# Filter rows interleaved over the partitions of a spectral filter and token MLP kernel, and the waits for loads moved ahead of the last two stores

## The chip, the cores and the metric

The kernel runs on one core of a Trainium2 chip. The metric is the device time of one launch in microseconds (us); lower is better. Names of engines: PE is TensorE (matmul; PEld is its weight load), DVE is VectorE, ACT is ScalarE, POOL is GpSimd, SP is SyncE, which here only issues DMAs (its queue is called SPq in the profile).

## The reference

Two blocks follow each other on one input of 2048 tokens by 512 channels, bf16. The first is a global filter: a 2D real FFT, a product with a complex weight, and the inverse FFT, added to the input. The second is a token-mixing MLP with a GELU. Layer norms go ahead of both (two of them in a row ahead of the MLP).

```python
def _A_ref(x, w_r, w_i):                       # x: (1, 2048, 512)
    X = rfft2(x.astype(float32), axes=(-2, -1))
    X = X * (w_r + 1j * w_i)                   # w: (2048, 257)
    return irfft2(X, s=(S, D), axes=(-2, -1)).astype(bfloat16)

def _B_ref(x, w1, b1, w2, b2):                 # w1: (2048, 1376), w2: (1376, 2048)
    h = _layernorm(x)
    u = gelu(einsum("bsd,sf->bdf", h, w1) + b1)
    return (einsum("bdf,fs->bds", u, w2) + b2).transpose(0, 2, 1)

h  = x + _A_ref(_layernorm(x), A_w_r, A_w_i)
h2 = h + _B_ref(_layernorm(h), B_w1, B_b1, B_w2, B_b2)
```

## The kernel before

Everything is matmuls with tables of sines and cosines. A token index is 16 p + s2, with p on the 128 partitions and s2 from 0 to 15.

- Stage f1 (lines 658 to 678) transforms over p, with the layer norm's factor folded into the table FS; stage f2 (681 to 689) transforms over the channels; stage x (692 to 709) transforms over s2 with the table M and multiplies by the filter. Stages f2, x and g1 run over u from 0 to 7, four groups g of frequencies per u (lines 727 to 731).
- In stage x, two DVE multiplications of 128 x 1024 per u (line 707) read the matmul's result from PSUM and the filter tiles Wr and Wi from SBUF, and write V. Stage g1 (712 to 725) transforms V back over s2 with the table R into PQ.
- Stages g2 and g3 (lines 743 to 756) transform back over channels and p, and line 758 adds the input to make H; lines 760 to 779 are the second layer norm, which gives HH; mm1 and mm2 (736 to 741, 809 to 817) are the MLP. Line 815 makes the output tile OUT on DVE, and a DMA per s2 stores it.

The filter tiles Wr and Wi hold [128 partitions, 32 groups, 257 channels] of bf16. A partition is a row of the spectrum: a pair (k2, s), a sign (the row of a positive frequency or of its mirror), and comp, the real or imaginary part that the row of data holds. The function `_row` (line 40) says which partition that is; the tables M and R are filled with it. Before the change, the rows of positive sign lie at partitions 0 to 63, those of negative sign and comp 0 at 64 to 95, and of negative sign and comp 1 at 96 to 127. Both comps need the same filter values, so every value is loaded twice.

The filter is loaded in three blocks of groups (0 to 8, 8 to 16, 16 to 32), for Wr and then for Wi in each (lines 584 to 597): one DMA for partitions 0 to 63, whose rows are contiguous in memory (8 or 16 groups of 514 bytes), and one for each of the two quarters of 32 partitions with the mirrored rows, which run backwards in memory and so consist of pieces of 514 bytes. In the first block two small loads (`z0`, `z1`) bring the group that has no mirror. That makes 22 DMAs, all on SP's queue, behind the input X, the tables FP and EM, and ahead of the table IF, the weights W1, the biases and W2.

The order of work is made by a planner in Python (`schedule`, line 289) when the kernel is built. Each operation has an estimated duration, a priority and dependencies; the planner puts the operations in an order for each engine. A DMA's duration is its bytes over a `rate` in bytes per ns (220 for the filter, 290 or 400 for others). Dependencies come from `cells` (line 207): it turns a piece of a tile into keys of 32 or 4 bytes and a block of 32 partitions, and writers and readers of the same key depend on each other. `gen_sync` (381) turns them into semaphores; a DMA gets one of 60 semaphores of the SP queue in turn, or one of 8 of the ACT queue. `emit` (427) writes the instructions. Right before the last store, it makes SP wait for the final value of every DMA semaphore but the one of that store (62 waits, line 440), and after the store for that one.

Of the kernel before, what the change touches and what calls it, by code (L numbers as in the profile page):

```python
# [10 lines left out]
NP = 128  # L11
# [26 lines left out]


def _row(sign, comp, k2, s):  # L40
    return 64 + comp * 32 + k2 * 2 + s if sign else (k2 * 2 + s) * 2 + comp


def _fwd_matrices(special):


    m = np.zeros((64, 2, 128), np.float64)
    for s, k2, kind, sign, k2o, so in _outputs(special):
        for n in range(16):
            w = np.exp(-1j * TWO_PI * n * k2 / 16)  # L50
            if kind == 3:
                w = w * np.exp(-1j * np.pi * n / 16)
            sg = -1j if kind == 1 else 1j
            comps = {0: ((0, 1.0), (1, 1j)), 1: ((0, 1.0), (1, 1j)), 2: ((0, 1.0),), 3: ((1, 1.0),)}[kind]
            for comp, uc in comps:
                for cs, us in ((0, 1.0), (1, sg)):
                    v = w * uc * us
                    m[n * 4 + comp * 2 + s, cs, _row(sign, 0, k2o, so)] += v.real
                    m[n * 4 + comp * 2 + s, cs, _row(sign, 1, k2o, so)] += v.imag
    return m  # L60


def _inv_matrices(special):

    r = np.zeros((128, 2, 128), np.float64)

    def col(pq, n, comp, s):
        return pq * 64 + n * 4 + comp * 2 + s

    for s, k2, kind, sign, k2o, so in _outputs(special):  # L70
        for n in range(16):
            e = np.exp(1j * TWO_PI * k2 * n / 16)
            if kind == 3:
                e = e * np.exp(1j * np.pi * n / 16)
            for wri in range(2):
                jw = 1.0 if wri == 0 else (-1j if kind == 1 else 1j)
                for comp, uc in ((0, 1.0), (1, 1j)):
                    z = jw * uc * e
                    rr = _row(sign, comp, k2o, so)
                    if kind >= 2:  # L80
                        r[rr, wri, col(0, n, kind - 2, 0)] += 2.0 * z.real
                        r[rr, wri, col(1, n, kind - 2, 0)] += -2.0 * z.imag
                    else:
                        q = 1j * z * (1.0 if kind == 0 else -1.0)
                        r[rr, wri, col(0, n, 0, s)] += z.real
                        r[rr, wri, col(0, n, 1, s)] += z.imag
                        r[rr, wri, col(1, n, 0, s)] += q.real
                        r[rr, wri, col(1, n, 1, s)] += q.imag
    return r
# [62 lines left out]
def lane_quantum(lane):  # L152
    return 16 if lane.startswith("dq") else 1
# [27 lines left out]
class Builder:  # L181
# [25 lines left out]
    def cells(self, ap):  # L207
        lo, size = self.tensors[ap.tensor.name]
        esz = dt.size(ap.dtype)
        dims = list(ap.ap)  # L210
        pstep, pn = dims[0]
        row = size // esz
        off = int(ap.offset)
        p0, f0 = divmod(off, row)
        offs = np.array([f0], dtype=np.int64)
        run = 1
        for step, n in dims[1:]:
            if n == 1:
                continue
            offs = (offs[:, None] + step * np.arange(n, dtype=np.int64)[None, :]).reshape(-1)  # L220
        b = lo + offs * esz
        small = size <= 1024
        cell = 4 if small else CELL
        c = np.unique(np.concatenate([b // cell, (b + esz - 1) // cell]))
        quads = range(p0 // 32, (p0 + pn - 1) // 32 + 1)
        return [(small, q * 131072 + int(x)) for q in quads for x in c]

    def op(self, name, engines, emit, ins=(), outs=(), dur=100.0, unit=None, pr=False, pw=False,
           first=False, last=False, prio=0, nbytes=0, is_dma=False, not_before=0.0, after=(), lat=None, rate=None):
# [197 lines left out]
    def emit(self, es):  # L427
        nc = self.nc
        sems = {lane: es.enter_context(nc.semaphore(f"sem_{lane}")) for lane in sorted(self.lane_count)}
        block = es.enter_context(nc.Block())  # L430
        sec = {"sp": "sync", "pe": "tensor", "act": "scalar", "dve": "vector", "pool": "gpsimd"}
        for sname in _STREAMS:
            ops = self.streams[sname]

            def section(eng, sname=sname, ops=ops):
                for k, o in enumerate(ops):
                    if sname == "sp" and k == len(ops) - 1:
                        for lane in sorted(self.lane_count):
                            if lane.startswith("dq") and lane != o.lane:
                                eng.wait_ge(sems[lane], lane_quantum(lane) * self.lane_count[lane])  # L440
                    for lane, v in o.waits:
                        eng.wait_ge(sems[lane], v * lane_quantum(lane))  # L442
                    ins = o.emit(sname, eng, o.unit.bank if o.unit is not None else None)
                    if o.increments:
                        ins.then_inc(sems[o.lane], lane_quantum(o.lane))
                if sname == "sp":
                    eng.wait_ge(sems[ops[-1].lane], lane_quantum(ops[-1].lane) * self.lane_count[ops[-1].lane])
                    eng.nop()
            getattr(block, sec[sname])(section)

# [63 lines left out]
def build_kernel(nc, A_x, A_w_r, A_w_i, B_w1, B_b1, B_w2, B_b2, out):  # L514
# [11 lines left out]
    Wx = (T["Wr"], T["Wi"])  # L526
# [7 lines left out]
    def dma(name, dst, src, nbytes, stream="sp", outs=(), ins=(), prio=0, nb=0.0, strided=False, after=(), rate=None):  # L534
        def emit(s, eng, bank):
            if strided:
                with nc.allow_non_contiguous_dma(reason="small bias gather"):
                    return eng.dma_start(dst, src)
            return eng.dma_start(dst, src)  # L539
        return K.op(name, stream, emit, ins=ins, outs=outs, nbytes=nbytes, is_dma=True, prio=prio, not_before=nb, after=after, rate=rate)  # L540
# [33 lines left out]
    ld_x(12, 16, "act")  # L574
    ld_fp(8, 16)
    dma("ld_EM", EM[:], cin["EM"][:, :], 6656 * 128, outs=[EM[:]], prio=29)
    def w_cells(w, p0, p1, h0, h1):

        res = [Wx[w][p0:p1, h1 - 1:h1, 0:240]]
        if h1 - h0 > 1:  # L580
            res.append(Wx[w][p0:p1, h0:h1 - 1, :])
        return res

    for g0, g1 in ((0, 8), (8, 16), (16, 32)):
        n = (g1 - g0) * 257
        for w, dram in ((0, A_w_r), (1, A_w_i)):
            dma(f"ld_w{w}p_{g0}", Wx[w][0:64, g0:g1, :], bass.AP(dram.tensor, g0 * 257, [[64 * 257, 32], [0, 2], [1, n]]), 64 * n * 2,
                outs=w_cells(w, 0, 64, g0, g1), prio=28, rate=220.0)
            h0 = max(g0, 1)
            for comp in range(2):  # L590
                p0, p1 = 64 + comp * 32, 96 + comp * 32
                if g0 == 0:
                    dma(f"ld_w{w}z{comp}", Wx[w][p0:p1, 0:1, :], bass.AP(dram.tensor, 32 * 257, [[64 * 257, 32], [1, 257]]), 32 * 514,
                        outs=w_cells(w, p0, p1, 0, 1), prio=28)
                dma(f"ld_w{w}m{comp}_{g0}", Wx[w][p0:p1, h0:g1, :],
                    bass.AP(dram.tensor, (64 - h0) * 257, [[64 * 257, 32], [-257, g1 - h0], [1, 257]]),
                    32 * (g1 - h0) * 514, outs=w_cells(w, p0, p1, h0, g1), prio=28, rate=220.0)
    B1s, B1f, B2s, B2f = (T[n] for n in ("B1s", "B1f", "B2s", "B2f"))
    dma("ld_IF", IF[:], cin["IF"][:, :, :, :], 1 << 20, outs=[IF[:]], prio=27)
    w1src = B_w1.rearrange("(p s2) f -> p s2 f", s2=NS2)  # L600
# [25 lines left out]
    for i0, i1 in ((0, 2), (2, 4), (4, 6), (6, 8), (8, 10), (10, 12), (12, 14), (14, 15), (15, 16)):  # L626
# [21 lines left out]
        for i in range(i0, i1):  # L648
# [3 lines left out]
                 lambda s, eng, bank, i=i, r=r: eng.tensor_scalar(FS[:, i, :, :], FP[:, i, :, :], r, None, op0=ALU.mult),  # L652
# [6 lines left out]
    for q in range(4):  # L659
        for b in range(2):  # L660
            unit = PsumUnit("f1", 2)
            for n in range(4):
# [3 lines left out]
                f = FS[:, n2, 1, :]  # L666
# [76 lines left out]
    for s2 in range(NS2):  # L743
# [33 lines left out]
        m, r = mv[:, s2, 0:1], T["rs2"][:, s2:s2 + 1]  # L777
        K.op(f"ln2_ap{s2}", "dve", lambda s, eng, bank, m=m, r=r, hs=hs, s2=s2: eng.tensor_scalar(HH[:, s2, :], hs, m, r, op0=ALU.subtract, op1=ALU.mult),  # L778
             ins=[hs, m, r], outs=[HH[:, s2, :]], dur=320.0, prio=9)
        for t in range(5):  # L780
# [5 lines left out]
         outs=[B1f[0:96, 10:11]], dur=80.0)  # L786
# [39 lines left out]
def bass_sequential_preLN__spectral_gfnet__mixer_token_mlp__prompt_kernel(  # L826
    nc,
    A_x,
    A_w_r,
    A_w_i,  # L830
    B_x,
    B_w1,
    B_b1,
    B_w2,
    B_b2,
    out,
):
    build_kernel(nc, A_x, A_w_r, A_w_i, B_w1, B_b1, B_w2, B_b2, out)
# [28 lines left out]
```

## Time and profile before

| | us |
|---|---|
| time, median of 3 runs (lowest to highest) | 147.34 (146.84 to 148.27) |
| span of the profiled run | 145.5 |
| PE busy | 124.7 (86%) |
| DVE busy | 81.0 (56%) |
| ACT busy | 64.3 (44%) |
| mean DMA rate over the span | 156 GB/s |

A time is about 2 us longer than the span that the profile covers. The busy time of engines is an average over stages with different limits, so the stages are read one by one. A slice of the page's second part is 3.6 us:

```profile
PE   0059879999197599999999999999999999999980
DVE  0489948994349659999600369744452423233330
PEclk9999999999869999999999999999999999999998
DMA  4999999999999999997000000000012121212121
```

Each digit is the busy share of a slice in tenths; PEclk is the clock granted to TensorE, and DMA the mean share of the 16 DMA engines. The first half of the DMA row is full, up to about 65 us; the stores at the end show as 1 and 2. The PE row is full from about 55 us to the end and uneven before.

### The profile page before, as it was taken

Reading aid. Unit: us, or ns where it says so; the run is one execution under the profiler, and the core shown is the slowest. Engines: PE = TensorE matmul, PEld = TensorE weight load, DVE = VectorE, ACT = ScalarE, POOL = GpSimd, SP = SyncE. Lnnn points to the kernel's source line nnn. Section 1 sums busy time; section 2 is a strip of 40 time slices with the busy share of each in tenths; the row PEclk is TensorE's granted clock in tenths of the full one; section 3 lists DMA queues with packets and bytes.
Section 4 is the critical chain, followed back from the end, with each engine's and each line's share of the span. In section 5 each row is a group of like instructions: output and inputs, shape, how many; then the busy total and the mean of one; then the engine's idle time right before and its main releaser. Section 6 shows DMA issues by size and latency. Waiting matters only on the chain.

```text
span 145.5 us, 2043 instructions
## 1 busy us (share of the span) xinstructions
PE 124.7 (86%) x754; PEld 77.7 (53%) x754; DVE 81.0 (56%) x169; ACT 64.3 (44%) x138; POOL 18.1 (12%) x49
## 2 busy tenths in 40 slices
PE   0059879999197599999999999999999999999980
PEld 0036757577155476666444444445666666666640
DVE  0489948994349659999600369744452423233330
ACT  4699963578054479998200597533410000000000
POOL 0077600000000000575800000000000000000000
PEclk9999999999869999999999999999999999999998
DMA  4999999999999999997000000000012121212121
GB/s 134 349 398 320 195 190 217 160 193 169 374 431 412 421 264 403 395 316 315 7 5 0 0 0 0 0 0 0 0 40 73 36 72 36 72 41 72 38 70 41
DMA packets 12122, 22.77 MB, mean 156 GB/s; under 512 B 2544, under 2 KB 8688, under 8 KB 11344
## 3 DMA queue, kind: packets, MB, share of 16 engines
q1 hardware_dynamic: 11680, 21.33, 49.6%
q10 hardware_dynamic: 432, 1.31, 2.6%
q8 instruction: 6, 0.10, 0.3%
q14 instruction: 4, 0.03, 0.1%
HBM read 20.54 MB, written 2.10 MB: 156 GB/s over the span
## 4 chain that ended last, share of the span: by engine, by line
PE 62%; SPq 14%; DMA 11%; DVE 9%; issue 1%; DVEq 0%
PE ps L544 62%; SPq L539 14%; DMA Wi<-in_A_w_i_dram 11%; DVE V L707 6%; DVE H L758 1%; DVE OUT L815 1%; DVE PQ L553 0%; DVE st_101 L764 0%; DVE HH L778 0%; DVE mv_102 L765 0%; DVEq L442 0%; DVE rs_104 L616 0%
## 5 line engine op out<-in xcount | busy, mean ns | idle before, releaser
L544 PE MATMUL ps<-HH,W_77 128*128 128x512 bf16 (+1 forms) x176 | 39.8, 379 | 0.2 <-DVE HH L778 0.2
L544 PEld LDWEIGHTS ps<-HH,W_77 128*128 128x128 bf16 (+1 forms) x176 | 17.6, 100 | 19.1 <-issue 0.4
L815 DVE SCALAR_TENSOR_TENSOR OUT<-ps,B2f,H 128x512 bf16<-128x512 f32 x16 | 12.0, 751 | 23.8 <-PE ps L544 23.8
L544 PE MATMUL ps<-FS,X 128*128 128x256 bf16 x64 | 10.3, 334 | 9.5 <-POOL FS L652 9.0
L544 PE MATMUL ps<-EM,V 128*128 128x128 bf16 x128 | 10.1, 225 | 4.6 <-DVE V L707 4.6
L544 PEld LDWEIGHTS ps<-FS,X 128*128 128x128 bf16 x64 | 7.2, 118 | 12.3 <-POOL FS L652 9.7
L552 ACT ACTIVATE PQ<-ps 128x512 bf16<-128x512 f32 x15 | 8.2, 598 | 10.3 <-PE ps L544 10.3
L544 PEld LDWEIGHTS ps<-EM,V 128*128 128x128 bf16 x128 | 8.1, 100 | 7.3 <-DVE V L707 5.6
L758 DVE TENSOR_TENSOR H<-ps,X 128x512 bf16<-128x512 f32 x16 | 10.4, 676 | 2.2 <-PE ps L544 2.2
L707 DVE TENSOR_TENSOR V<-ps,Wr 128x1024 bf16<-128x1024 f32 x8 | 9.5, 1220 | 3.5 <-PE ps L544 3.5
L707 DVE TENSOR_TENSOR V<-ps,Wi 128x1024 bf16<-128x1024 f32 x8 | 9.5, 1218 | 3.4 <-DMA Wi<-in_A_w_i_dram 3.4
L544 PE MATMUL ps<-EM,Y 128*128 128x256 bf16 x64 | 9.3, 276 | 1.3 <-DVE Y L553 1.0
L544 PE MATMUL ps<-EM,PQ 128*128 128x256 bf16 x64 | 9.1, 272 | 0.9 <-DVE PQ L553 0.9
L552 ACT ACTIVATE EO<-ps 128x512 bf16<-128x512 f32 x16 | 8.8, 590 | 1.7 <-PE ps L544 1.5
L552 ACT ACTIVATE CS<-ps 128x512 bf16<-128x512 f32 x14 | 7.8, 605 | 3.4 <-PE ps L544 3.4
L544 PE MATMUL ps<-CS,EM 128*128 128x512 bf16 (+1 forms) x34 | 9.2, 397 | 0.1
L622 ACT ACTIVATE JK<-X 128x512 bf16<-128x512 bf16 x14 | 8.6, 614 | 1.2 <-DMA X<-in_A_x_dram 1.2
L544 PE MATMUL ps<-EO,IF 128*128 128x256 bf16 (+1 forms) x48 | 9.1, 308 | 0.0
L622 ACT ACTIVATE JK<-H,nb_98 128x512 bf16<-128x512 bf16 x11 | 7.9, 719 | 2.6 <-DVE H L758 2.4
L643 DVE BATCH_NORM_STATS2 st_94<-X 128x6 f32<-128x512 bf16 x9 | 5.8, 676 | 5.5 <-DMA X<-in_A_x_dram 5.4
L544 PEld LDWEIGHTS ps<-EM,Y 128*128 128x128 bf16 x64 | 5.9, 100 | 3.5 <-issue 1.5
L544 PEld LDWEIGHTS ps<-EM,PQ 128*128 128x128 bf16 x64 | 6.2, 98 | 2.0 <-ACT PQ L552 1.0
(85 smaller groups left out, 189.0 us busy)
## 6 DMA issues: line engine op xcount, KB each, us to landing
W_77<-in_B_w_dram SPq DMA_DIRECT2D x4, 1376.0 KB, 20.3
out_dram<-OUT SPq DMA_DIRECT2D x16, 128.0 KB, 1.7
Wr<-in_A_w_r_dram SPq DMA_DIRECT2D x4, 257.0 KB, 13.0
Wi<-in_A_w_i_dram SPq DMA_DIRECT2D x4, 257.0 KB, 13.6
X<-in_A_x_dram SPq DMA_DIRECT2D x2, 512.0 KB, 7.4
IF<-c_IF SPq DMA_DIRECT2D x1, 1024.0 KB, 15.7
EM<-c_EM SPq DMA_DIRECT2D x1, 832.0 KB, 12.4
Wr<-in_A_w_r_dram SPq DMA_DIRECT2D x1, 514.0 KB, 12.0
```

What stands on the lines that cost most here:

```text
L539: return eng.dma_start(dst, src)
L544: return eng.matmul(outf(bank), lhsT, rhs, start=start, stop=stop, **({"skip_group_check": True} if skip else {}))
L552: return eng.activation(dst, srcf(bank), ACT.Copy)
L622: K.op(name, "act", lambda s, eng, bank: eng.activation(jk, src, func, accum_out=acc, **kw), ins=[src] + ([bias] if bias is not None else ...
L643: K.op(f"ln1_st{i}", "dve", lambda s, eng, bank, st=st, i=i: eng.bn_stats(st, X[:, i, :]), ins=[X[:, i, :]], outs=[st], dur=600.0, prio=20)
L707: return eng.tensor_tensor(ov, src, wv, ALU.mult)
L758: K.op(f"h_{s2}", "dve", lambda s, eng, bank, xs=xs, hs=hs: eng.tensor_tensor(hs, ps[:, bank, :], xs, ALU.add), ins=[xs], outs=[hs], dur=6 ...
L815: K.op(f"fin{s2}", "dve", lambda s, eng, bank, dst=dst, bia=bia, hs=hs: eng.scalar_tensor_tensor(dst, ps[:, bank, :], bia, hs, op0=ALU.add ...
```

## The change

Three edits go together.

1. `_row` now puts row k = 2 k2 + s, sign and comp at partition 4 k + 2 sign + comp. The tables M and R follow it.
2. The filter loads follow: every load writes 32 partitions in steps of four, from 0, 1, 2 or 3, over the whole height of SBUF. The rows of positive sign, which were one load of 64 partitions, become two loads of 32, one for each comp. There are 28 filter loads instead of 22. [...] The planner's rate for them goes from 220 to 330. `cells` now keys a piece by its block of 32 partitions and the partition modulo four, so that the loads of a block don't depend on each other.
3. The waits for all DMA semaphores come before the last but one store instead of before the last one, and leave out the semaphores of the last four stores, which SP waits for after the last store.

```diff
 def _row(sign, comp, k2, s):
-    return 64 + comp * 32 + k2 * 2 + s if sign else (k2 * 2 + s) * 2 + comp
+    return 4 * (k2 * 2 + s) + 2 * sign + comp
...
-        quads = range(p0 // 32, (p0 + pn - 1) // 32 + 1)
-        return [(small, q * 131072 + int(x)) for q in quads for x in c]
+        step = pstep // row if pn > 1 else 1
+        parts = p0 + step * np.arange(pn)
+        base = np.unique((parts // 32) * 4 + parts % 4)
+        keys = (base[:, None] * 131072 + c[None, :]).reshape(-1) * 2 + small
+        return keys.tolist()
...
+                last = {o.lane for o in ops[-4:]}
                 for k, o in enumerate(ops):
-                    if sname == "sp" and k == len(ops) - 1:
+                    if sname == "sp" and k == len(ops) - 2:
                         for lane in sorted(self.lane_count):
-                            if lane.startswith("dq") and lane != o.lane:
+                            if lane.startswith("dq") and lane not in last:
                                 eng.wait_ge(sems[lane], lane_quantum(lane) * self.lane_count[lane])
...
                 if sname == "sp":
-                    eng.wait_ge(sems[ops[-1].lane], lane_quantum(ops[-1].lane) * self.lane_count[ops[-1].lane])
+                    for lane in sorted(last):
+                        eng.wait_ge(sems[lane], lane_quantum(lane) * self.lane_count[lane])
                     eng.nop()
...
     for g0, g1 in ((0, 8), (8, 16), (16, 32)):
         n = (g1 - g0) * 257
+        h0 = max(g0, 1)
         for w, dram in ((0, A_w_r), (1, A_w_i)):
-            dma(f"ld_w{w}p_{g0}", Wx[w][0:64, g0:g1, :], bass.AP(dram.tensor, g0 * 257, [[64 * 257, 32], [0, 2], [1, n]]), 64 * n * 2,
-                outs=w_cells(w, 0, 64, g0, g1), prio=28, rate=220.0)
-            h0 = max(g0, 1)
             for comp in range(2):
-                p0, p1 = 64 + comp * 32, 96 + comp * 32
+                dma(f"ld_w{w}p{comp}_{g0}", Wx[w][comp:NP:4, g0:g1, :], bass.AP(dram.tensor, g0 * 257, [[64 * 257, 32], [1, n]]), 32 * n * 2,
+                    outs=w_cells(w, comp, g0, g1), prio=28, rate=330.0)
+                p0 = 2 + comp
                 if g0 == 0:
-                    dma(f"ld_w{w}z{comp}", Wx[w][p0:p1, 0:1, :], bass.AP(dram.tensor, 32 * 257, [[64 * 257, 32], [1, 257]]), 32 * 514,
-                        outs=w_cells(w, p0, p1, 0, 1), prio=28)
-                dma(f"ld_w{w}m{comp}_{g0}", Wx[w][p0:p1, h0:g1, :],
+                    dma(f"ld_w{w}z{comp}", Wx[w][p0:NP:4, 0:1, :], bass.AP(dram.tensor, 32 * 257, [[64 * 257, 32], [1, 257]]), 32 * 514,
+                        outs=w_cells(w, p0, 0, 1), prio=28)
+                dma(f"ld_w{w}m{comp}_{g0}", Wx[w][p0:NP:4, h0:g1, :],
                     bass.AP(dram.tensor, (64 - h0) * 257, [[64 * 257, 32], [-257, g1 - h0], [1, 257]]),
-                    32 * (g1 - h0) * 514, outs=w_cells(w, p0, p1, h0, g1), prio=28, rate=220.0)
+                    32 * (g1 - h0) * 514, outs=w_cells(w, p0, h0, g1), prio=28, rate=330.0)
```

More of the change, by code (lines that the diff above doesn't have):

```diff
@@ L576, in build_kernel, with w_cells @@
     dma("ld_EM", EM[:], cin["EM"][:, :], 6656 * 128, outs=[EM[:]], prio=29)
-    def w_cells(w, p0, p1, h0, h1):
-        res = [Wx[w][p0:p1, h1 - 1:h1, 0:240]]
+    def w_cells(w, p0, h0, h1):
+        res = [Wx[w][p0:NP:4, h1 - 1:h1, 0:240]]
         if h1 - h0 > 1:
-            res.append(Wx[w][p0:p1, h0:h1 - 1, :])
+            res.append(Wx[w][p0:NP:4, h0:h1 - 1, :])
         return res
```

## The prediction

> **What bounds the kernel now.** I read the page first: PE is busy for 86% of the span and carries 62% of the chain that ended last; the SP queue (14%) and one DMA, the imaginary filter Wi (11%), come next. Then the chain of waits in order of time, to see where in the kernel those two lie. Columns: start, duration, what.
>
> ```profile
> 22.38 15.54 DMA Wi<-in_A_w_i_dram
> ...
> 38.11 1.24 DVE V L707
> 39.34 0.05 issue
> 39.39 2.65 PE ps L544 x11
> 42.04 0.02 issue
> 42.06 1.24 DVE V L707
> 43.30 0.02 issue
> 43.32 5.76 DVE V L707 x5
> ...
> 49.78 0.70 DVE PQ L553
> 50.49 0.14 issue
> 50.62 2.03 PE ps L544 x16
> ...
> 55.95 85.38 PE ps L544 x424
> ```
>
> The kernel is paced by PE from 50.62 (stage g2 starts) to the end; before that, the last filter load lands at 37.92 and holds a multiplication of stage x. The timeline of that stage shows the hold (idle time and releaser in brackets).
>
> ```profile
> 38.11 1.23 DVE L707 TENSOR_TENSOR V<-ps,Wi 128x1024 bf16<-128x1024 f32 x1 [3.39 <-DMA Wi<-in_A_w_i_dram]
> 39.39 0.93 PE L544 MATMUL ps<-EM,V 128*128 128x128 bf16 x7 [3.12 <-DVE V L707]
> 42.06 1.23 DVE L707 TENSOR_TENSOR V<-ps,Wr 128x1024 bf16<-128x1024 f32 x1 [2.73 <-PE ps L544]
> ```
>
> DVE loses 3.39 us to the load and then 2.73 us more, because PE had stood for 3.12 us and came back slow. Next, windows for what DMA and clock did (last three columns: granted clock, DMA share, GB/s).
>
> ```profile
> 12.90:23.00 10.10, 8.64 (x68) 6.55 (x67) 7.89 (x24) 8.45 (x17) 3.71 (x7) 1.00 1.13 195
> 23.00:30.00 7.00, 6.75 (x58) 4.29 (x57) 6.54 (x7) 3.23 (x6) 0.00 (x0) 1.00 1.17 185
> 30.00:36.70 6.70, 6.18 (x76) 4.65 (x72) 4.40 (x4) 5.74 (x12) 0.00 (x0) 1.00 1.12 182
> 37.50:50.00 12.50, 8.77 (x77) 5.79 (x77) 8.41 (x8) 5.27 (x10) 0.00 (x0) 0.86 1.01 424
> 39.40:42.20 2.80, 2.80 (x14) 1.63 (x15) 0.14 (x1) 0.63 (x2) 0.00 (x0) 0.50 1.00 421
> ```
>
> From 12.9 to 36.7 the queues hold only filter loads, all 16 DMA engines are busy, and yet they move 182 to 195 GB/s; right after, with IF and W1 (128 partitions), the same engines move 424. The last row is the half clock after PE's pause. The packet records of the trace split the filter loads in two: 4112- and 8224-byte packets (the positive-frequency rows, partitions 0 to 63) take a median of 309 and 620 ns, 13.3 B/ns, against 416 ns for W1's 11008 bytes, 26.5 B/ns. So the first kind runs at exactly half speed although its packets are long. The 514-byte packets (mirrored rows, partitions 64 to 95 and 96 to 127) take 55 ns, 9.3 B/ns.
>
> Last, the end of the span: the final store.
>
> ```profile
> 139.75 3.11 SPq L539 DMA_DIRECT2D out_dram<-OUT  x2
> ...
> 142.53 0.33 SPq L539 DMA_DIRECT2D out_dram<-OUT  x1
> ```
>
> DVE is done with the last output at 141.35 + 0.75 = 142.10, and the store starts at 142.53. The store before it started at 139.75, 0.03 us after its own DVE instruction (138.97 + 0.75).
>
> [...]
>
> **The change, part by part.**
>
> *Rows moved to 4k + 2 sign + comp.* The tables M and R are filled for the new order on the host; shapes and counts of matmuls stay. Cost: nothing.
>
> *Filter loads.* Each load now writes 32 partitions in steps of four (c, c+4, ... c+124)[...]. Bytes (4.21 MB: 8 x 257 + 2 x 514 + 4 x 128.5 + 4 x 112.4 + 4 x 16.1 KB) and row lengths stay. Long rows: 256 x 309 ns and 128 x 620 ns over 16 engines is 10.2 of the 23.8 us; at 424 GB/s instead they take 5.0. Short rows: the other 13.6 us. [...] So the filter takes 11.8 to 18.7 us instead of 23.8. It ends at 24.7 to 31.6, and with the 1.1 us that the last load now needs from its last packet (36.8) to landing (37.92), it is there at 26 to 32.7. I take the middle, 29. The multiplication that waits for it is ready at 34.74, when the Wr product before it ends. Either end removes the wait.
>
> *Six more load issues* (28 for 22): an issue took 0.42 to 0.65 us while the queue was empty (3.16 to 7.3), so about 3 us of SP time. Behind them on SP are IF, W1, biases and W2. SP is being held by full queues in this stage anyway (IF's issue took 3.65 us, the bias issues 20.88), so this hides under the transfers: 28 x 0.6 from 3.16 puts the last issue at 20, before the transfers end at 24.7 or later.
>
> *The stage after the wait is gone.* Nine multiplications from 23.75 to 34.72 ran without waiting for a load: 10.97 / 9 = 1.22 us each, stalls included. Seven remain: 8.5 us, so the last ends at 43.26 instead of 49.07. PE must keep up: after 36.28 it has 77 matmuls left, 56 at 0.064 (twenty in 1.28), 12 at 0.215 and 9 at 0.13 (eight in 1.04), 7.4 us at full clock, so 43.7. Hence the two tie. From last product to g2 is 1.55 us now (49.07 to 50.62) and stays: g2 starts at 44.8, 5.8 us earlier. PE no longer pauses, so the half clock (2.8 us, worth 1.4) is inside this number.
>
> *From g2 to the end* PE is busy for 90.49 of 90.71 us, so all of it moves with the start. IF and W1 come behind the filter in the same queue: filter end + 2.5 us (1.05 MB) + 13.3 us (5.6 MB) at 424 GB/s is 45 for my middle and 47.5 at worst, the first quarter of W1 about ten us sooner, while the first matmul that needs it moves from about 56 to 50. Hidden. W2 is needed after 100.
>
> *Waits at the last stores.* Before the last store SP waits for 62 semaphores, among them, fourth in order, the one of the store before, which lands 1.7 us after its issue: 141.45. The other 58 take until 142.53, 19 ns each. With the change 59 waits stand ahead of the last but one store, at 137.7 (its predecessor issued), 1.1 us before 138.9, and that store has nothing to do until 139.72. Nothing else is queued on SP, and nobody waits for it. The last store then starts 0.04 us after DVE: 0.39 us saved. Three extra waits at the very end are on stores already landed.
>
> *The planner* (rate 330 for 220 in its estimates, dependencies by partition modulo four) orders all instructions anew. Its effect on PE I take as nothing within 1 us either way, since totals are fixed and PE is full after g2.
>
> **Sum**: 5.8 + 0.39 = 6.2 us; 147.34 - 6.2 = 141.2 us.
>
> **Rivals.**
> 1. *[...]something takes the wait's place* (13%): the new order makes PE or DVE wait between stages, or short rows gain nothing and a middle group of loads comes late. For: DVE and PE tie in that stage (10.46 and 10.63 busy of 10.97), so a poor order costs at once. Against: even the slow end of the loads leaves 2 us. Some 2 to 3 us of the gain lost: 143 to 144.5.
> 2. *The loads are no faster* (7%). [...] For: 514-byte rows at 9.3 B/ns are below even half speed. Against: 4112-byte rows at exactly half. Only the end's 0.39 us remains: 147.0.
> 3. *Slower* (5%): scattered partitions or more loads in the queue lengthen the filter by 10%, 2.4 us, all of it on the chain: 147.34 + 2.4 - 0.39 = 149.4. Against: rows and bytes unchanged.
> 4. *The last store also lands sooner* (within the forecast): it needs 2.6 us, the median store 1.7; packet records show an instruction fetch of 0.72 us on one DMA engine beside it. If the new order of waits moves that fetch, up to 0.9 us more: 140.3.
>
> **How the numbers follow.** Forecast, with its fourth case, 75%: 140.0 to 142.4. Rival 1 to 144.5, rivals 2 and 3 beyond 146. The range 139.9 to 144.6 leaves out rivals 2, 3 and a little on either side. Faster by over 1% (below 145.9): forecast and rival 1, 0.88; same 0.07; slower 0.05.
>
> **What would show it.** Right: filter loads at 270 GB/s or more; no wait of V for Wi; no half clock between 36 and 42; g2 at 44 to 46; a last store issued 0.04 us after DVE. Wrong: GB/s near 190 in that stage, or a wait of V or PE of over 1 us on another releaser before g2, or a stretch from g2 to the end longer than 91 us.

## The result, and the profile after

The changed kernel takes 142.03 us (median of 4 runs, 141.91 to 142.17), the kernel before beside it 147.09 us (145.48 to 148.27). The ratio is 0.9692, with a 95% interval of 0.9612 to 0.9772: faster. Where runs are compared by their clock below, those more than 1.5% above the fastest run of the same kernel are left out. The forecast was 141.2 us, with a range of 139.9 to 144.6.

The chain of waits after (start, duration, what), over the stretch where the load of Wi stood before:

```profile
31.52 5.92 PE ps L549 x62
37.43 0.02 issue
37.45 1.24 DVE V L712
38.69 0.02 issue
38.71 5.76 DVE V L712 x5
...
45.18 0.70 DVE PQ L558
45.88 0.14 issue
46.02 2.03 PE ps L549 x16
...
51.34 85.38 PE ps L549 x424
```

The only DMA in the chain is now the first load of X, at the very start. Stage g2 starts at 46.02 instead of 50.62. What follows is the same to the hundredth: 85.38 us of PE, as before. Lines have moved by five: matmuls, 544 before, are now 549, the multiplications 712 for 707, and DMAs 544 for 539.

The timeline of stage x:

```profile
34.71 1.23 DVE L712 TENSOR_TENSOR V<-ps,Wi 128x1024 bf16<-128x1024 f32 x1
35.99 0.56 PE L549 MATMUL ps<-EM,V 128*128 128x128 bf16 x7
37.45 1.23 DVE L712 TENSOR_TENSOR V<-ps,Wr 128x1024 bf16<-128x1024 f32 x1 [1.52 <-PE ps L549]
```

The multiplication by Wi that waited 3.39 us starts at once, and PE runs on at full clock (granted clock 1.00; seven matmuls in 0.56 us instead of 0.93). But the next multiplication still waits for PE, 1.52 us of the 2.73. That part of the wait was not the load's.

Windows of the filter loads and of what follows them (last column: GB/s):

```profile
12.60:20.00 7.40, 5.97 (x49) 4.35 (x47) 6.83 (x22) 6.79 (x16) 3.80 (x8) 1.00 1.07 347
20.00:25.30 5.30, 4.71 (x41) 3.54 (x42) 3.52 (x5) 2.47 (x4) 0.00 (x0) 1.00 1.11 354
25.50:40.00 14.50, 13.96 (x140) 9.68 (x138) 12.30 (x12) 10.94 (x21) 0.00 (x0) 1.00 1.02 426
```

The filter moves at about 350 GB/s for 182 to 195 before. The packet records say the same: 4112-byte packets take a median of 164 ns (25 B/ns) for 309, and 514-byte packets 28 ns for 55. From first to last packet the filter takes 12.8 us (24.1 before). Its last load is issued at 21.1 and lands 4.5 to 4.8 us later, by 25.9, nine microseconds before it is needed.

The last store (first line: duration of its issue in ns, then its start in us; second: issue to landing):

```profile
L544 SPq DMA_DIRECT2D out_dram<-OUT x1: 332/332/332, 137.5 to 137.5; - x1
DMA to landing us min/median/max: 1.9/1.9/1.9
```

DVE ends at 136.74 + 0.75 = 137.49, and the issue starts 0.03 us later (0.43 us before), and the store lands in 1.9 us for 2.6. From DVE's end to the end of the span it was 3.4 us and is 2.4.

The spans differ by 145.5 - 139.9 = 5.6 us: 4.6 ahead of g2 and 1.0 at the end. Every compute engine executes the same instructions in the same order as before; only SP's queue differs. So the new estimates of the planner moved nothing else.

### The profile page after: what moved, and what is told of

It is laid out like the page before. It is cut to its first block, busy times and chain, and to the rows that moved or that the text cites. A ratio compares the mean times of both kernels' runs of the same rounds, so it can differ in the third digit from the quotient of the medians.

```text
span 139.9 us, 2050 instructions
## 1 busy us (share of the span) xinstructions
PE 122.4 (87%) x754; PEld 76.6 (55%) x754; DVE 81.3 (58%) x169; ACT 64.0 (46%) x138; POOL 18.1 (13%) x49
## 3 DMA queue, kind: packets, MB, share of 16 engines
q10 hardware_dynamic: 432, 1.31, 2.7%
## 4 chain that ended last, share of the span: by engine, by line
PE 75%; DVE 13%; ACT 4%; DMA 3%; POOL 2%; issue 1%; POOLq 0%
PE ps L549 75%; DVE V L712 5%; DMA X<-in_A_x_dram 3%; DVE st_94 L648 2%; POOL FS L657 2%; ACT JK L627 2%; ACT PQ L557 1%; DVE H L763 1%; DVE Y L558 1%; DVE OUT L820 1%; DVE PQ L558 1%; DVE st_101 L769 0%; ACT CS L557 0%; DVE mv_95 L650 0%; DVE FS L657 0%
## 5 line engine op out<-in xcount | busy, mean ns | idle before, releaser
L820 DVE SCALAR_TENSOR_TENSOR OUT<-ps,B2f,H 128x512 bf16<-128x512 f32 x16 | 12.0, 750 | 23.8 <-PE ps L549 23.8
L549 PE MATMUL ps<-FS,X 128*128 128x256 bf16 x64 | 9.4, 315 | 10.2 <-POOL FS L657 10.2
L549 PEld LDWEIGHTS ps<-FS,X 128*128 128x128 bf16 x64 | 6.7, 112 | 12.6 <-POOL FS L657 9.7
L549 PE MATMUL ps<-EM,V 128*128 128x128 bf16 x128 | 9.6, 220 | 1.6 <-DVE V L712 1.5
L549 PE MATMUL ps<-CS,EM 128*128 128x512 bf16 (+1 forms) x34 | 8.3, 367 | 0.2 <-ACT CS L557 0.2
L806 DVE TENSOR_TENSOR Q_51<-U_50 128x512 bf16<-128x512 bf16 x3 | 1.3, 423 | 10.5 <-ACT U_50 L804 10.5
```

The costliest lines, as they stand in the source:

```text
L549: return eng.matmul(outf(bank), lhsT, rhs, start=start, stop=stop, **({"skip_group_check": True} if skip else {}))
L806: K.op(f"gelu{t}_q", "dve", lambda s, eng, bank, U=U, Q=Q: eng.tensor_tensor(Q, U, U, ALU.mult), ins=[U], outs=[Q], dur=350.0, prio=5)
L820: K.op(f"fin{s2}", "dve", lambda s, eng, bank, dst=dst, bia=bia, hs=hs: eng.scalar_tensor_tensor(dst, ps[:, bank, :], bia, hs, op0=ALU.add ...
```

## Experiments

Each was timed in alternation with the kernel before. That kernel varies by some 3 us from run to run, and its mean clock varies with it: where no window of half clock fell into the stages before g2 (mean 0.997 to 1.0), it took 145.4 to 146.6, with one (0.985 to 0.988) 146.8 to 148.0. Where it matters, runs of the same mean clock are compared.

**e1: the changed kernel again.**

> The changed kernel once more, as the measure for the three runs beside it. Expected 141.9 to 142.2 us, as its four runs so far; stage g2 starts at 46.0 us, the last store is issued 0.04 us after DVE.

142.20 us (141.97 to 142.44), and in its profile g2 starts at 46.20. This is the measure for e2 to e4.

**e2: each load within one half of the partitions.**

```diff
-    return 4 * (k2 * 2 + s) + 2 * sign + comp
+    return 64 * sign + 2 * (k2 * 2 + s) + comp
...
-dma(..., Wx[w][comp:NP:4, g0:g1, :], ...)
+dma(..., Wx[w][comp:64:2, g0:g1, :], ...)
...
-p0 = 2 + comp
+p0 = 64 + comp
...
-Wx[w][p0:NP:4, h0:g1, :]
+Wx[w][p0:NP:2, h0:g1, :]
```

> The changed kernel with rows at 64 sign + 2 k + comp: the same 28 loads of 32 partitions, the same bytes, packets and order on every engine, but each load steps by two within one half of the partitions. Theory 1[...]: the filter moves at 180 to 200 GB/s again, 4112-byte packets take about 310 ns, a V multiplication waits about 3 us for Wi, PE falls to half clock, and the time is 145.5 to 147 us (the kernel before less the 1 us gained at its end). Theory 2 (the gain came from cutting the 64-partition load in two, or from more loads in flight): 330 GB/s or more, no wait, 142 us. In between (250 GB/s): no wait, 142 us, and packets of about 230 ns.

142.93 us (142.28 to 143.17). None of the three expectations had this. Windows and the critical multiplication of this kernel:

```profile
12.60:20.00 7.40, 6.14 (x49) 4.39 (x47) 6.83 (x22) 6.79 (x17) 3.86 (x8) 1.00 1.12 237
20.00:25.00 5.00, 4.35 (x34) 3.17 (x35) 3.22 (x5) 2.17 (x4) 0.00 (x0) 1.00 1.17 224
25.00:30.00 5.00, 4.75 (x47) 3.25 (x47) 4.82 (x5) 3.07 (x7) 0.00 (x0) 1.00 1.12 196
...
35.69 1.23 DVE L712 TENSOR_TENSOR V<-ps,Wi 128x1024 bf16<-128x1024 f32 x1 [1.06 <-DMA Wi<-in_A_w_i_dram]
```

Theory 1 is right about long packets: 4112 bytes take 314 ns, half speed. It was wrong about the time. The short packets take 44 ns (55 before, 28 in steps of four), the filter is 2.4 us shorter than before (21.7 for 24.1 from first to last packet), and that is nearly the whole wait: 1.06 us are left of 3.39. PE pauses for 0.79 us only, and no run shows the window of half clock (mean clock 0.996 to 1.0). What remained from the change was the number of loads and their order: positive and mirrored rows, lower and upper half, now alternate.

**e5: each load within one half, loads not alternating.** As e2, with the two positive loads next to each other:

```diff
             for comp in range(2):
                 dma(f"ld_w{w}p{comp}_{g0}", ...)
+            for comp in range(2):
                 p0 = 64 + comp
```

> As the kernel[...] (28 loads, steps of two), but the two loads of positive rows stand next to each other and ahead of the mirrored ones, as in the kernel before; there they alternated between the lower and the upper half of the partitions. Theory 1 (alternating loads let packets for the two halves overlap[...]): the filter falls to 180 to 205 GB/s throughout, Wi is waited for by 2.5 to 3.5 us, PE goes to half clock in most runs, time 144.5 to 147 us. Theory 2 (it was the cut of the loads[...]): as with alternation, 142.5 to 143.2 us.

On average 146.59 us where the mean clock was 0.988 (eight runs) and 145.14 where it was 1.0 (four), within half a microsecond of e6 below, which has the 22 loads of the kernel before and the same end. Windows and the wait (us in all, times, longest):

```profile
12.60:20.00 7.40, 5.86 (x49) 4.31 (x47) 6.83 (x22) 6.79 (x16) 3.72 (x8) 1.00 1.12 203
20.00:25.00 5.00, 4.49 (x37) 3.31 (x38) 3.22 (x5) 2.17 (x4) 0.00 (x0) 1.00 1.16 205
25.00:30.00 5.00, 4.75 (x47) 3.25 (x45) 4.81 (x5) 3.07 (x7) 0.00 (x0) 1.00 1.17 174
...
DVE V L713 <- DMA Wi<-in_A_w_i_dram: 3.1, 1, 3.1
```

So with each load within one half, the cut of the loads brings nothing that shows, and their order brings the gain: from e5 to e2, with the same 28 loads, the rate at the start goes from 203 to 237 GB/s, short packets from 55 to 44 ns, and the wait from 3.1 to 1.06 us.

The packet records say more. Long packets go to the lower half of the partitions, short ones to the upper. Both kinds are in flight together for 92% of the filter's time in e2, 53% in e5 and 69% in the kernel before. There, a short packet takes a median of 68 ns with no long one beside it, and 47 to 55 with one. Why alternation helps is not shown: alternating halves here also means alternating long and short rows, and no run separates the two. In the changed kernel a short packet takes 28 ns with or without a long one beside it, which speaks against the row lengths.

**e9: the kernel before, its loads alternating.**

```diff
-            dma(f"ld_w{w}p_{g0}", Wx[w][0:64, g0:g1, :], ...)
             for comp in range(2):
+                dma(f"ld_w{w}p{comp}_{g0}", Wx[w][comp:64:2, g0:g1, :], ...)
                 p0, p1 = 64 + comp * 32, 96 + comp * 32
```

(`cells` keys by partition modulo four as in the change, so that the two pieces don't depend on each other. Compute engines keep their order.)

> The kernel before, its rows[...], plan and end, with one edit: the load of the 64 positive rows is cut into its two comps (steps of two), and the pieces alternate with the mirrored loads: positive 0, mirrored 0, positive 1, mirrored 1. Theory 1 (alternation between the two halves of the partitions[...], since the stage needs the last load by 34.7 us only): a wait for Wi of 0.8 to 1.5 us for 3.4, no half clock, g2 near 47, time 143.3 to 144.2 us[...]. Theory 2 (the new row order matters in another way): 146 to 147.5 us.

143.60 us (142.67 to 143.84); ratio 0.9728 (0.9641 to 0.9816). Rows, the half that each load writes and the end are those of before. The timeline:

```profile
34.13 1.22 DVE L710 TENSOR_TENSOR V<-ps,Wr 128x1024 bf16<-128x1024 f32 x1 [0.32 <-PE ps L547]
35.53 1.22 DVE L710 TENSOR_TENSOR V<-ps,Wi 128x1024 bf16<-128x1024 f32 x1 [0.18 <-DVE V L710]
38.28 1.23 DVE L710 TENSOR_TENSOR V<-ps,Wr 128x1024 bf16<-128x1024 f32 x1 [1.52 <-PE ps L547]
```

The wait for Wi has gone, with a load that is split and moved in the queue and nothing else. But it has gone narrowly: Wi lands at 35.31 (37.92 before), and the multiplication by Wr ahead of it ends at 35.35, 0.64 us later than in the kernel before, because in this run the stage as a whole started that much later (24.38 for 23.75); why is open. Stage g2 starts at 46.84.

Alternation by itself is worth 4.0 us (147.6, the kernel before beside it, to 143.6), the avoided half clock included; the one run beside it without half clock took 145.94, 2.3 more. With alternation in place, the spread of each load over both halves, which the change was made for, adds 0.6 us (e9 to e3 below, 143.01, which has the spread and the same old end; their runs overlap, and they were timed on two chips) or 0.7 with the new end (e2 to e1). What the spread would be worth without alternation was not run: no kernel here has spread loads that are grouped.

**e3: the waits back ahead of the last store.**

```diff
-                last = {o.lane for o in ops[-4:]}
+                last = {o.lane for o in ops[-1:]}
...
-                    if sname == "sp" and k == len(ops) - 2:
+                    if sname == "sp" and k == len(ops) - 1:
```

> The changed kernel with all DMA waits but one back ahead of the last store, as in the kernel before. Theory 1 (the prediction's: waits and the landing of the store before hold the last issue): the last store is issued 0.4 us late, lands 1.7 to 1.9 us later, +0.4 us, 142.4. Theory 2 (a fetch of instructions, which falls where SP has run through its long list of waits, holds the issue and then one DMA engine): issue 0.4 late and landing 2.6 instead of 1.9 us, +1.0 us, 143.0. Theory 3 (the end is hidden): no difference.

143.01 us (142.56 to 144.14), 0.8 more than e1. Its last store:

```profile
L544 SPq DMA_DIRECT2D out_dram<-OUT x1: 341/341/341, 137.8 to 137.8; - x1
DMA to landing us min/median/max: 2.2/2.2/2.2
```

DVE ended at 137.35: the issue is some 0.4 us late. The landing lies between those of theories 1 and 2, the median of the times at theory 2's.

**e6: the new end alone, on the kernel before.** The second diff of the change without the first.

> The kernel before with the new place of the waits alone, loads and rows untouched. Theory 1 (the end is worth 0.8 to 1.0 us, independent of the loads): last store issued 0.04 us after DVE and landing in 1.7 to 1.9 us; 0.6 to 1.0 us less than the kernel before at the same clock (about 146.6 where the mean clock is 0.988, about 145 where it is 1.0). Theory 2 (no gain of its own): as before.

Over all runs the ratio is 0.9986 (0.9949 to 1.0023), which settles nothing, since the waits for Wi scatter more than the end is worth. At the same mean clock the averages are 146.62 for 147.21 (0.988, nine and thirteen runs) and 145.60 for 146.07 (0.997 to 1.0, five and fifteen runs): 0.5 to 0.6 us, a little less than theory 1 had. Its last store is issued on time and lands in 2.0.

**e8 and e10: few waits, in the old and in the new place.**

```diff
+                stores = {o.lane for o in ops if o.name.startswith("st_")}
...
-                            if lane.startswith("dq") and lane not in last:
+                            if lane in stores and lane not in last:
```

> The changed kernel with the waits back ahead of the last store, but only those on the stores' own semaphores (15 for 62; the loads have been waited for by their readers). Theory 1 (the length of the list holds the last store: 31 wait instructions of two semaphores at 62 ns and a pause of 0.45 us make 2.43 us, more than the 2.38 us between two stores less 0.33 for the issue): 8 instructions take 0.5 us, the last store is issued 0.04 us after DVE, time 141.8 to 142.3. Theory 2 (the landing of the store before, which is waited for in that place, holds it): issued 0.4 us late, 142.6 to 143.0.

> The changed kernel, its waits in their new place ahead of the last but one store, but only those on the stores' semaphores (12 for 59). Theory 1 (what counts is when SP fetches its last instructions: with the long list the fetch falls into the list, ahead of the last stores; without it, beside the last store): the last store is issued on time but lands in 2.3 to 2.6 us, time 142.7 to 143.2, as with few waits in the old place. Theory 2 (the place of the waits counts): 141.9 to 142.4, landing in 1.7 to 1.9 us.

e8, in the old place: 143.07 us (142.98 to 143.45). e10, in the new one: 142.37 (142.32 to 143.47). The last store of e8, then of e10:

```profile
L545 SPq DMA_DIRECT2D out_dram<-OUT x1: 332/332/332, 137.6 to 137.6; - x1
DMA to landing us min/median/max: 2.5/2.5/2.5
```

```profile
L545 SPq DMA_DIRECT2D out_dram<-OUT x1: 332/332/332, 137.5 to 137.5; - x1
DMA to landing us min/median/max: 1.8/1.8/1.8
```

A short list hardly holds the issue (0.12 us after DVE in e8), but e8 gains nothing: its store lands late. In e8 the packet records show a fetch of instructions (8192 bytes, 0.61 us) 0.2 us after the store's first packet, and one part of the store ends 0.7 us after the others (in the kernel before, a fetch of 0.72 us begins at 143.30, 15 of the store's 16 landings come by 143.86, the last at 144.63); in e10 a fetch begins just as the last packet of the store goes out. In eleven profiles here the last store lands in 2.2 to 2.6 us where a fetch runs beside most of its packets (before, e3, e7, e8, e9) and in 1.8 to 2.0 where it begins only with the last of them (after, e1, e2, e5, e6, e10). That the fetch delays the store is the author's reading of these eleven. The records also give a likely reason why a late issue costs twice: in every profile the fetch begins 1.16 to 1.31 us after DVE's last output. The packets of a store issued on time run from 0.86 to 1.36 us after it and are nearly all out; those of a store issued 0.4 us late begin at 1.25. In e8 the store is 0.1 us late and the fetch 0.13 us early, against e10. What starts the fetch is open. Theory 1 of e10 is refuted, since a short list alone doesn't bring the fetch beside the store.

**e4: stage f2 ahead of g1 in the plan.**

```diff
-                   unit, b == 0, b == 1, par == 0 and b == 0, 10, 256)
+                   unit, b == 0, b == 1, par == 0 and b == 0, 12.5, 256)
...
-        evac(f"f2_{G}_ev", ..., unit, 512, 10)
+        evac(f"f2_{G}_ev", ..., unit, 512, 12.5)
```

> The changed kernel with a higher planning priority of stage f2 (12.5 for 10, its evacuations too), which places f2 ahead of g1 where both are ready. Theory 1 (the 1.52 us for which DVE still waits for PE at the sixth group is due to the order of instructions on PE, and not to the amount of work): that wait is gone, g2 starts at 44 to 44.7, time 140.2 to 140.8. Theory 2 (PE has no slack in that stage, so the wait moves elsewhere): g2 at 45.5 to 46.5, time 141.5 to 142.5. If the earlier multiplications came to wait for filter loads, it would be slower: Wi's last load lands at about 25.7 and is needed from 33, so this is not expected.

140.01 us (139.90 to 140.20), ratio to the kernel before 0.9516 (0.9447 to 0.9585), 2.2 us less than e1: better than both kernels.

```profile
33.24 2.36 DVE L712 TENSOR_TENSOR V<-ps,Wr 128x1024 bf16<-128x1024 f32 x2 [0.18 <-PE ps L549]
35.52 2.35 DVE L712 TENSOR_TENSOR V<-ps,Wi 128x1024 bf16<-128x1024 f32 x2
37.86 2.36 DVE L712 TENSOR_TENSOR V<-ps,Wr 128x1024 bf16<-128x1024 f32 x2
40.13 2.35 DVE L712 TENSOR_TENSOR V<-ps,Wi 128x1024 bf16<-128x1024 f32 x2
...
44.03 1.58 PE L549 MATMUL ps<-EM,PQ 128*128 128x256 bf16 x13 [0.88 <-DVE PQ L558]
```

Multiplications run back to back, and g2 starts at 44.03. The wait of 1.52 us was the order of instructions on PE, where g1 stood ahead of the matmuls of the next groups.

**e7: the same, on the kernel before.**

> The kernel before, slow loads and old end, with stage f2 at priority 12.5. Theory 1 (loads and order are two separate losses: after Wi has landed at about 37.9, DVE no longer waits 2.73 us for PE, because the matmuls of the next groups are already done): g2 starts 1.5 to 2.7 us earlier, time 144.5 to 146. Theory 2 (behind the late load the order is of no use): 147 to 147.6. In both, the wait for Wi is as long or longer, 3.4 to 4.5 us.

144.79 us over all runs (142.62 to 146.12), ratio 0.9811 (0.9767 to 0.9855). At mean clock 0.988 the average is 144.5 for 147.2, but of two runs only; at 0.995 to 1.0 it is 143.4 (six runs) for 146.1 (fifteen). The profile still has the wait for the load, and no wait for PE behind it:

```profile
38.79 2.36 DVE L707 TENSOR_TENSOR V<-ps,Wi 128x1024 bf16<-128x1024 f32 x2 [2.90 <-DMA Wi<-in_A_w_i_dram]
41.15 2.36 DVE L707 TENSOR_TENSOR V<-ps,Wr 128x1024 bf16<-128x1024 f32 x2
43.42 2.35 DVE L707 TENSOR_TENSOR V<-ps,Wi 128x1024 bf16<-128x1024 f32 x2
```

So load and order are two separate losses, some 2.7 us for the order here and 2.2 with the change. Two points were missed: the wait is 2.90 us, not 3.4 or more, and g2 starts at 47.32, 3.3 us earlier than in the kernel before. PE paused for 2.91 us, but this run had no window of half clock, so its g2 can't be compared with that of the profile before.

## Why the prediction was right, and where it was wrong

The time lay 0.8 us above the forecast, inside its range. Of the signs that it named for being right all came true, one barely: filter loads at 347 GB/s and more, no wait of V for Wi, no half clock, g2 at 46.02 (44 to 46), the last store on time. But so did one that it named for being wrong: a wait of over 1 us on another releaser before g2, the 1.52 us of DVE for PE. The first rival had such a wait, as one that the new order of instructions would bring; it had been there before.

- *The filter loads.* Right on the packets: in steps of four the long ones are nearly as fast as those of W1 (25 and 26.5 B/ns), and the short ones at twice their speed, the fast end of the range of 11.8 to 18.7 us (12.8 measured). That loads in steps of four would move as fast as those of 128 partitions was the author's estimate, and so was the range for the short rows, from half of their 13.6 us to all of it; the trace before showed neither. The 10.2 us for long rows can't be had from the medians beside it, which give 9.9; the averages of the records (319 and 637 ns) give 10.2.
- *The cause of the gain.* The packet times bear out the prediction's cause, loads that are faster in steps of four, but it is not the only one in the change, and whether it would be enough alone was not run. It named one lever, the spread of each load over both halves. Nothing in the trace before tested alternation; both halves were in flight for 69% of the filter's time. e9 tests it: each load within its half as before, alternating, and the wait is gone. Alternation shortens the filter by 9% (e5 to e2, 23.8 to 21.7 us), and since the stage needed the last load only 3.4 us sooner, that is worth 4.0 us and leaves 0.6 to 0.7 for the spread. The prediction did see that far less than a doubled rate would do ("Either end removes the wait"), but never asked what else in the diff could bring that. So the time does not show that the spread was needed.
- *"Seven remain: 8.5 us."* The term of the sum that was mis-sized. The seven multiplications took from 34.71 to 44.47, 9.76 us. The average of the first nine was carried over, although the trace had a wait of 2.73 us for PE among the seven, which the prediction put down to the load and the half clock. Of it, 1.52 us was order (e4). Its tie with PE (43.7) counted PE's work at full clock, not the order in which PE would do it. The 5.8 us became 4.6.
- *"19 ns each", 0.39 us at the end.* Too small, with a wrong working. By the trace's records two semaphores share one wait instruction, one every 62 ns, and with a pause of 0.45 us the 31 of them last 2.4 us, as long as the time between two stores. In the new place they hold the last store but one until 0.34 us after DVE (135.46 for 135.11), not on time as forecast, where nobody waits for it. The end brought 1.0 us in the profile because the late landing went too, the fourth rival; by time it is 0.5 (e6) to 0.8 us (e3).
- *The planner.* "Nothing within 1 us" holds: the order on every compute engine is unchanged.

The errors of -1.2 and +0.6 partly cancel: 6.2 forecast, 5.6 in the profile, 5.1 between the medians; among the runs of the kernel before is one of 145.48, in the range of those that escape the window of half clock. That the time came so near the forecast is in part luck.

## What to carry to other kernels

When a load releases a stage, ask how much earlier it must land, and then for the cheapest edit that gives so much: here two microseconds from the order of loads in the queue did most of what the whole change of the loads did. A diff that moves data to other partitions may reorder its transfers too, as this one did, so test the order alone. And a wait that follows a late load need not be all the load's: see whether the instruction it waited for had been placed behind others.

## What the runs showed of the hardware

- Packets of 4112 bytes for 32 partitions in steps of four move at 25 B/ns (164 ns, after), nearly as fast as the 11008-byte ones of W1 for 128 partitions (416 ns before, 26.5), against 13 for 32 partitions in steps of two within one half (314 ns, e2) or 64 in a row (309 ns, before).
- Rows of 514 bytes take 28 ns a packet (18 B/ns) where each load steps by four over both halves (after), 55 where it lies within one (before), and 44 within one when loads for the two halves alternate (e2). Packets for the two halves are in flight together for 92% of the filter's time in e2, 53% in e5 and 69% before.
- The window of half clock lasts 3.41 us in the record of the kernel before. Pauses of PE of 3.12 us (before) and 2.86 us (e5) brought one, pauses of 2.91 us (e7) and 0.79 us (e2) none, so the length of the pause alone doesn't decide. Runs of the kernel before with one window took 1.1 us longer on average (147.21 for 146.07), of which the longer wait for the load may be a part.
- Instruction fetches of 8192 bytes stand among the DMA packets (0.72 us at 143.30 before, 0.42 us at 138.81 after). Where one ran beside most packets of the last store, these took 0.9 to 1.3 us from first to last, and 0.5 where none did.
